# Re-timing block sums and gate-weight sums in the second half of layer one of a linear-attention and gMLP kernel

## Chip, cores and metric

The kernel runs on one core of one Trainium2 chip. The metric is device time in microseconds of one execution. Engines go by the profile's names: PE is TensorE, DVE is VectorE, ACT is ScalarE, POOL is GpSimd, and SP is the engine whose queue issues most of the transfers (DMAs).

## The reference

Four blocks follow each other on a 2048 x 512 tensor in float32: attention block A, gMLP block B, and both once more with the same weights. "Layer one" is the first A and B.

```python
x = x + _A_ref(_layernorm(x), A_wqkv, A_wo)
x = x + _B_ref(_layernorm(x), B_w_in, B_w_sp, B_b_sp, B_w_out)
...
def _A_ref(x, wqkv, wo):          # H = 32 heads of 16
    q, k, v = ...                 # x @ wqkv
    pq, pk = phi(q), phi(k)       # where(t > 0, t + 1, exp(t)) + 1e-6
    kv = einsum("bhsd,bhse->bhde", pk, v)
    z = einsum("bhsd->bhd", pk)
    o = einsum("bhqd,bhde->bhqe", pq, kv) / (einsum("bhqd,bhd->bhq", pq, z)[..., None] + 1e-6)
    return o.reshape(B, S, D) @ wo
def _B_ref(x, w_in, w_sp, b_sp, w_out):    # Fh = 896
    z = gelu(x @ w_in)
    z1, z2 = z[..., :Fh], layernorm(z[..., Fh:])
    g = einsum("ts,bsf->btf", w_sp, z2) + b_sp[None, :, None]
    return (z1 * g) @ w_out
```

## The kernel before

**Numbers.** Each float32 matrix is held as two halves: `high` (line 134, ACT) rounds it, `low` (137, DVE) takes the rest. A product is three matmuls (`mm3`, 147): high by high, high by low, low by high.

**Block products.** The large product with `w_sp` (2048 x 2048) and part of the product with `w_in` are computed with seven products of blocks in place of eight, so sums of blocks are needed as operands. The *block sums* of `w_sp` are made by `Sums` (1172): for each of 16 pieces it loads three 128 x 512 tiles (a21, a22, a11), makes three sums on POOL, a21 + a22, a21 + a11 and (a21 + a22) + a11 (`add`, 1206), and stores them to DRAM for the later stage `P4`. `fetch` (1183) issues the three loads, `store` (1197) the three stores, `tick` (1210) does one piece's share of a step. Eight of the pieces are made in the loop below, the rest in layer one's `P4`, where `tick` is called as well. The *gate-weight sums* are those of `w_in`'s first half: `Make` (203) handles three groups g. From the step `MAKE_AT[g]` on it loads two tiles, one step later makes four half-width adds on DVE (`add`, lines 215 to 218), then splits one tile on ACT and DVE in each of two steps and stores each a step later (`store`, 226).

**The loop.** The second half of layer one's attention and the first product of its gMLP run in `P2.run` (1081), in steps s of one row tile (128 rows) each. In the order in which they are recorded, step s does the following from s = 6 on:

- issue loads of x for row s + 1 and of the turned query row (`qturn.load`), and the stores of the last sums (`sums.store()`)
- b(s): DVE transposes the query row (line 330), ACT and DVE split it
- den: three short DVE operations (805 to 807) for row s + 2
- c(s - 1): 12 matmuls, then DVE adds the residual (846) and takes statistics (264, 266), whose root is taken on POOL (268 to 273)
- `a2_mul` (814, DVE), `c3`: ACT normalises the row (279), which is stored turned (yt, through `xturn`); `a` (793) is a multiplication on POOL
- d(s - 2): DVE transposes the turned row that was loaded in the step before, ACT and DVE split it into a quarter of a `qd` tile (`d_high`, `d_low`). In steps 14 and on `d_high` comes before `c3`
- e(s - 3): 24 matmuls of width 448, GELU on ACT (902); e4(s - 4) normalises an earlier row on ACT (279), and DVE takes a difference (913) when that row is below 8; e3 takes statistics, with a root on POOL
- f: up to two groups of 12 matmuls of width 512, each with a GELU on ACT (927) and a store of its output. There are two groups in most steps, one in steps 9 and 13, none in 14
- from step 14 on `side` gives six or twelve block-product matmuls (993 to 995) a step
- `make.step(s)`, one split of the gate weights (`w1.piece`, POOL takes the rest until step 7), then `sums.tick` and `xturn.load(s - 1)`

e(s - 3) in step s reads what d wrote in step s - 1, and c(s - 1) reads what b wrote in step s - 1.

**What sets the order.** The kernel is recorded by hand: each engine runs its instructions in the order written, and waits on semaphores. SP issues its transfers in the same way, so a transfer that waits holds all behind it. A transfer from SP also waits, beside its data, for the eighth before it.

**Where things lie.** Tiles `pg` (pages, 128 x 512) come from 23 slots, the one that was given back longest ago first, `lag` putting a page further back. A `z` tile of a row holds its query row first, then, by `ztag`, a sum's tile ("sum"), a GELU output ("out"), a turned row ("turn") and at last the row's z. `TOKEN_TICKS` names the steps in which sums are made and the z tile that takes the first of the three loaded tiles; the other two are pages. `SPARE_TAGS` names the z tile for the second GELU output of a step; without an entry it is a page.

Before, `tick(s)` stands at the end of step s: it stores what is made, loads the tiles for step s + 1 if that is in `TOKEN_TICKS`, and makes the sums of step s. The loads of a step thus stand in SP's queue ahead of `xturn.load(s - 1)`, and POOL makes the sums of step s behind all its other work of that step:

```python
w1.piece(True)
w1.fetch()
if self.L == 0:
    sums.tick(s, TOKEN_TICKS)
self.xturn.load(s - 1)
```

Of the kernel before, what the change touches and what calls it, by code (L numbers as in the profile page):

```python
# [25 lines left out]
PHI_EPS = 1e-6  # L26
DEFER = 6
STORE, POOL = 6, 3
TOKEN_TICKS = {at: (at,) for at in (5, 6, 8, 9, 11, 12, 13, 14)}
SPARE_TAGS = {6: 7, 8: 7, 9: 10, 11: 10, 14: 15, 16: 15}  # L30
MIX_TICKS = (2, 4, 7, 8, 10, 12, 14, 16, 20, 21, 23, 24, 26, 27, 29, 30, 32, 34, 35, 37, 38, 39, 40, 41)
MIX_UNITS = (11, 15, 18, 20, 25, 31, 36, 40), (1, 3, 5, 7, 9, 11, 13, 15)
MAKE_AT = 5, 8, 11
ROW_UNITS = range(1, 9)
INNER_UNITS = range(47, 55, 2)
FIRST_AT = ("N1", 4), ("N1", 7), ("N2", 1), ("N2", 2), ("N2", 4), ("N1", 10)
# [54 lines left out]
def mixer_kernel(ctx: ExitStack, tc: tile.TileContext, x_in, wqkv, wo_d, win1_d, win2_d, wsp_d, bsp_d, wout_d,  # L91
# [111 lines left out]
    class Make:  # L203
# [29 lines left out]
        def step(self, i):  # L233
            for g in range(3):
                at = i - MAKE_AT[g]
                if at == 0:
# [98 lines left out]
    class P1:  # L335
# [227 lines left out]
        def run(self):  # L563
            side = deque()
            for w in (self.wo, self.win2):
                side.extend([w] * len(w.pieces))
            if self.L == 0:
                self.first(side)
            else:
                self.second(side)  # L570
# [201 lines left out]
    class P2:  # L772
# [308 lines left out]
        def run(self, sums):  # L1081
            w1 = self.win1
            own = inner["N1"]
            make = Make() if self.L == 0 else None
            for s in range(1, NT + 3):
                self.loadx(s + 1)
                self.qturn.load(s + 1)
                if self.L == 0:
                    sums.store()
                if s in self.qturn.by_pe:  # L1090
                    self.c(s - 1)
                    self.b_high(s)
                    self.c2(s - 1)
                    self.b_low(s)
                    self.c_stats(s - 1)
                    if s >= 2:
                        self.d_high(s - 2)
                        self.d_low(s - 2)
                    self.p1.late()
                    self.c3(s - 1)  # L1100
                    self.a2(s + 2)
                    self.p1.late_phi()
                    self.a(s + 3)
                elif s - 2 in self.xturn.by_pe:
                    self.b_high(s)
                    self.c(s - 1)
                    self.c2(s - 1)
                    self.c_stats(s - 1)
                    self.a2_den(s + 2)
                    self.b_low(s)  # L1110
                    self.a2_mul(s + 2)
                    self.d_high(s - 2)
                    self.d_low(s - 2)
                    self.c3(s - 1)
                    self.a(s + 3)
                else:
                    if s < NT:
                        self.b_high(s)
                    self.a2_den(s + 2)
                    if s < NT:  # L1120
                        self.b_low(s)
                    if s <= NT:
                        self.c(s - 1)
                        self.c2(s - 1)
                        self.c_stats(s - 1)
                    if s == NT:
                        quads.put(*self.W2)
                        pages.put(self.zbc)
                    self.a2_mul(s + 2)
                    sooner = s >= 14  # L1130
                    if sooner and s <= NT + 1:
                        self.d_high(s - 2)
                    if s <= NT:
                        self.c3(s - 1)
                    self.a(s + 3)
                    if s <= NT + 1:
                        if not sooner:
                            self.d_high(s - 2)
                        self.d_low(s - 2)
                if s >= 15:  # L1140
                    self.block_sums()
                if 4 <= s <= 6:
                    self.e3(s - 4)
                if 5 <= s <= 7:
                    self.e4(s - 5)
                if s > 6:
                    self.e4(s - 4)
                if s >= 3:
                    self.e(s - 3)
                    self.e2(s - 3)  # L1150
                if s >= 6:
                    self.e3(s - 3)
                self.f(s + 2)
                self.f(SPARE_TAGS.get(s) if self.L == 0 else None)
                self.side(s)
                if self.L == 0:
                    make.step(s)
                elif s == 5:
                    own.begin(2)
                elif 6 <= s:  # L1160
                    own.staged()
                self.fq.extend(self.fnext)
                self.fnext = []
                w1.piece(True)
                w1.fetch()
                if self.L == 0:
                    sums.tick(s, TOKEN_TICKS)
                self.xturn.load(s - 1)
            self.win2.free()


    class Sums:
# [37 lines left out]
        def tick(self, i, at):  # L1210

            self.store()
            if i + 1 in at:
                self.fetch(at[i + 1] if isinstance(at, dict) else ())
            if i not in at:
                return
            k, j, fourth = self.todo.popleft()
            if fourth:
                s2, a12 = self.raw.popleft()
                self.add(4, k, j, a12, s2, a12, s2)  # L1220
            else:
                a21, a22, a11 = self.raw.popleft()
                self.add(1, k, j, a22, a21, a22)
                self.add(3, k, j, a21, a21, a11)
                self.add(2, k, j, a11, a22, a11)
# [641 lines left out]
    sums = Sums()  # L1867
# [45 lines left out]
```

## Time and profile before

| | |
|---|---|
| median of 3 runs | 1369.9 us (1369.87 to 1370.38) |
| the profiled execution | 1370.94 us |
| its span, first to last instruction | 1369.2 us |
| mean granted TensorE clock | 0.999 |
| DMA traffic | 310.18 MB, mean 227 GB/s |
| sums made in the loop (line 1207) | 24 of 1.3 to 1.4 us |

The span is one execution as the hardware profiler saw it, the time of the run is a little longer than it. A group or timeline row names line, engine, operation, output and inputs by the program's tile names, and in brackets the idle time of the engine before it with what ended it. A row of a table by stretches gives its length and the busy time of PE, PE's weight loads, DVE, ACT and POOL with the number of instructions, then the granted clock, the DMA engines' busy share and GB/s.

### The profile page before, as it was taken

The numbers are of one execution on the slowest core, as the hardware profiler recorded it, in microseconds if no ns is written. First come the engines' busy times: TensorE is split into PE (matmuls) and PEld (weight loads), VectorE is DVE, ScalarE is ACT, GpSimd is POOL, SyncE is SP. The second block draws the span as 40 slices with busy tenths as digits, with TensorE's granted clock in tenths as the row PEclk, the third lists the DMA queues.
The fourth block names the chain that finished last, engine by engine and source line by source line (L and its number), as shares of the span: only waits on it lengthen the run. The fifth ranks groups of instructions, "written<-read, shape, count | busy, mean of one in ns | idle before, by whom it ended". The sixth has DMA issues, their size and how long they took to land.

```text
span 1369.2 us, 18313 instructions
## 1 busy us (share of the span) xinstructions
PE 1358.0 (99%) x6087; PEld 1132.8 (83%) x6087; DVE 1030.3 (75%) x1582; ACT 638.2 (47%) x1021; POOL 470.9 (34%) x551
## 2 busy tenths in 40 slices
PE   9999999989999999999999999999999999999998
PEld 7888888878888888878888888888888888888887
DVE  7985888777855888886678768887767798978642
ACT  6775544436542343432456655444455534533310
POOL 2333474463144237426421133633230011412340
PEclk9999999999999999999999999999999999999999
DMA  5762388886698988895686533666668798568652
GB/s 180 236 214 88 123 277 272 272 270 195 213 303 281 307 270 282 274 376 181 216 260 201 189 106 115 209 200 208 192 196 279 226 336 322 188 198 304 228 184 90
DMA packets 184496, 310.18 MB, mean 227 GB/s; under 512 B 15696, under 2 KB 67920, under 8 KB 180304
## 3 DMA queue, kind: packets, MB, share of 16 engines
q1 hardware_dynamic: 172736, 262.73, 59.0%
q0 software_dynamic: 8064, 39.85, 8.2%
q10 hardware_dynamic: 3600, 6.42, 1.3%
q8 instruction: 48, 0.79, 0.2%
q14 instruction: 48, 0.39, 0.1%
HBM read 211.68 MB, written 97.26 MB: 226 GB/s over the span
## 4 chain that ended last, share of the span: by engine, by line
PE 76%; DVE 3%; DMA 3%; ACT 1%; issue 1%; POOL 0%; SPq 0%; DVEq 0%; ACTq 0%; POOLq 0%
PE bank L151 12%; PE bank L150 12%; PE bank L149 12%; PE bank L1613 9%; PE bank L1615 9%; PE bank L1614 9%; PE bank L1544 3%; PE bank L1546 3%; PE bank L1547 3%; PE bank L995 1%; PE bank L993 1%; PE bank L994 1%; DMA qd<-n 1%; DMA pg<-qt 0%; DVE st L264 0%
## 5 line engine op out<-in xcount | busy, mean ns | idle before, releaser
L1613 PE MATMUL bank<-qd,pg 128*128 128x512 f32 x544 | 211.6, 389 | 0.0
L1614 PE MATMUL bank<-qd,pg 128*128 128x512 f32 x544 | 211.6, 389 | 0.0
L1615 PE MATMUL bank<-qd,pg 128*128 128x512 f32 x544 | 211.6, 389 | 0.0
L1460 DVE TENSOR_TENSOR qd<-qd,qd 128x1024 fp32r<-128x1024 f32 x104 | 144.4, 1388 | 70.3 <-ACT qd L1451 70.2
L1451 ACT ACTIVATE qd<-qd 128x1024 fp32r<-128x1024 f32 x104 | 110.1, 1058 | 137.5 <-DVE qd L1460 42.5
L151 PE MATMUL bank<-qd,pg 128*128 128x512 f32 x380 | 148.6, 391 | 0.5 <-DVE pg L138 0.5
L135 ACT ACTIVATE pg<-pg 128x512 fp32r<-128x512 f32 (+1 forms) x146 | 89.4, 621 | 121.4 <-DVE pg L330 46.4
L268 POOL TENSOR_SCALAR rs<-mv 128x1 f32<-128x1 f32 x95 | 42.3, 446 | 267.5 <-DVE mv L266 253.3
L1635 POOL TENSOR_TENSOR bg<-bg,pg 128x512 f32<-128x512 f32 x56 | 92.2, 1657 | 109.5 <-DMA pg<-z 104.0
L138 DVE TENSOR_TENSOR pg<-pg,pg 128x512 fp32r<-128x512 f32 (+1 forms) x143 | 111.2, 778 | 15.1 <-ACT pg L135 13.8
L1615 PEld LDWEIGHTS bank<-qd,pg 128*128 128x128 f32 x544 | 102.1, 188 | 21.3
L1614 PEld LDWEIGHTS bank<-qd,pg 128*128 128x128 f32 x544 | 102.1, 188 | 21.3
L1613 PEld LDWEIGHTS bank<-qd,pg 128*128 128x128 f32 x544 | 102.1, 188 | 21.0
L1207 POOL TENSOR_TENSOR pg<-pg,pg 128x512 f32<-128x512 f32 x48 | 72.2, 1505 | 135.4 <-DMA pg<-in_wsp_dram 93.2
L149 PE MATMUL bank<-qd,pg 128*128 128x512 f32 x284 | 110.9, 390 | 0.1
L150 PE MATMUL bank<-qd,pg 128*128 128x512 f32 x284 | 110.6, 389 | 0.0
L330 DVE STREAM_TRANSPOSE pg<-pg 128x512 f32<-128x512 f32 x79 | 86.3, 1092 | 16.9 <-DMA pg<-yt 11.2
L149 PE MATMUL bank<-bg,qd 128*128 128x448 f32 x256 | 95.1, 372 | 3.9 <-ACT qd L135 3.6
L151 PE MATMUL bank<-bg,qd 128*128 128x448 f32 x256 | 94.5, 369 | 0.2
L150 PE MATMUL bank<-bg,qd 128*128 128x448 f32 x256 | 94.3, 368 | 0.0
L1544 PE MATMUL bank<-qd,pg 128*128 128x512 f32 x224 | 87.5, 390 | 0.5 <-DMA qd<-n 0.5
L1546 PE MATMUL bank<-qd,pg 128*128 128x512 f32 x224 | 87.4, 390 | 0.3 <-DVE qd L1460 0.3
(220 smaller groups left out, 3194.0 us busy)
## 6 DMA issues: line engine op xcount, KB each, us to landing
qd<-s SPq DMA_DIRECT2D x64, 512.0 KB, 4.1
qd<-n POOLq DMA_DIRECT2D x32, 1024.0 KB, 8.3
pg<-in_wsp_dram SPq DMA_DIRECT2D x91, 256.0 KB, 4.7
qd<-in_wsp_dram SPq DMA_DIRECT2D x40, 512.0 KB, 4.4
s<-pg SPq DMA_DIRECT2D x56, 256.0 KB, 4.7
pg<-z SPq DMA_DIRECT2D x56, 256.0 KB, 4.0
n<-pg SPq DMA_DIRECT2D x55, 256.0 KB, 4.6
x<-pg SPq DMA_DIRECT2D x48, 256.0 KB, 2.7
```

Of the source, the lines that this page charges most:

```text
L138: nc.vector.tensor_sub(l, src, h.bitcast(F32))
L149: nc.tensor.matmul(out, ah, bh, start=start, stop=False)
L150: nc.tensor.matmul(out, ah, bl, start=False, stop=False)
L151: nc.tensor.matmul(out, al, bh, start=False, stop=stop)
L1451: nc.scalar.activation(wh, r, AF.Copy)
L1460: nc.vector.tensor_sub(wl, r, wh.bitcast(F32))
L1544: m(out[i], h[:, o, f], w[:, o, 0], start=first and name in ("P1", "P2", "P5"), stop=False, skip_group_check=True)
L1546: m(out[i], h[:, o, f], w[:, o, 1], start=False, stop=False, skip_group_check=True)
L1613: m(out, h[:, o], w[:, 0, j, :], start=start, stop=False, skip_group_check=True)
L1614: m(out, h[:, o], w[:, 1, j, :], start=False, stop=False, skip_group_check=True)
L1615: m(out, l[:, o], w[:, 0, j, :], start=False, stop=stop, skip_group_check=True)
L1635: nc.gpsimd.tensor_tensor(u, u, z1, op=OP.mult)
```

## The change

Three constants change, and the order at two places of the loop.

- `TOKEN_TICKS`: sums are made in steps 5 to 12, one piece a step, where it was 5, 6, 8, 9, 11, 12, 13 and 14.
- `Sums.tick` is cut in two: the new `Sums.sum` makes the sums. The loop calls it in the middle of step s, behind `a` and d and ahead of e4 and e3, so that POOL has them between `a` and the statistics of e3.
- The loads for the sums of step s + 1 are issued by the loop itself at the end of step s, behind `xturn.load(s - 1)` where they stood ahead of it. The stores stay at the start of the next step.
- `SPARE_TAGS` loses steps 6, 8, 9 and 11: z tiles 7 and 10 now take sums' tiles, and the second GELU output of steps 6, 8 and 11 is a page (step 9 has only one).
- `MAKE_AT`: 5, 8, 11 becomes 5, 7, 9. Make's loads are issued in steps 5, 7 and 9, its adds fall in steps 6, 8 and 10 (before 6, 9, 12), its splits in 7 and 8, 9 and 10, 11 and 12 (before 7 and 8, 10 and 11, 13 and 14), its last store in step 13 (before 15).

In `P4` of layer one `tick` is called as before and does the same as before. The matmuls and their order are the same.

```diff
-TOKEN_TICKS = {at: (at,) for at in (5, 6, 8, 9, 11, 12, 13, 14)}
-SPARE_TAGS = {6: 7, 8: 7, 9: 10, 11: 10, 14: 15, 16: 15}
+TOKEN_TICKS = {at: (at,) for at in range(5, 13)}
+SPARE_TAGS = {14: 15, 16: 15}
-MAKE_AT = 5, 8, 11
+MAKE_AT = 5, 7, 9
@@ in P2.run, after d
+                if self.L == 0:
+                    sums.sum(s, TOKEN_TICKS)
                 if s >= 15:
                     self.block_sums()
@@ in P2.run, at the end of a step
                 w1.piece(True)
                 w1.fetch()
-                if self.L == 0:
-                    sums.tick(s, TOKEN_TICKS)
                 self.xturn.load(s - 1)
+                if self.L == 0 and s + 1 in TOKEN_TICKS:
+                    sums.fetch(TOKEN_TICKS[s + 1])
@@ class Sums, in tick
             self.store()
             if i + 1 in at:
-                self.fetch(at[i + 1] if isinstance(at, dict) else ())
+                self.fetch()
+            self.sum(i, at)
+
+        def sum(self, i, at):
+
             if i not in at:
                 return
             k, j, fourth = self.todo.popleft()
```

## The prediction

> **What bounds the kernel now.** I read the page first, then TensorE's idle time row by row, then engine times cut at the steps of the changed loop (`P2.run`, layer one), then the queue and VectorE around each loss.
>
> ```profile
> span 1369.2 us, 18313 instructions
> PE 1358.0 (99%) x6087; PEld 1132.8 (83%) x6087; DVE 1030.3 (75%) x1582; ACT 638.2 (47%) x1021; POOL 470.9 (34%) x551
> ```
>
> TensorE is idle for 1369.2 - 1358.0 = 11.2 us in all, so a schedule change that leaves every matmul in place can win only that and time lost to a slow clock. Next, the steps; each row starts at the first matmul of c in steps 8 to 15 (columns: length, then busy time of PE, PEld, DVE, ACT, POOL, clock, DMA share, GB/s).
>
> ```profile
> 205.51:218.56 13.05, 13.05 (x61) 11.27 (x60) 9.85 (x18) 7.58 (x13) 4.97 (x8) 1.00 0.71 236
> 218.56:228.90 10.34, 10.34 (x50) 9.02 (x49) 9.21 (x14) 2.98 (x6) 5.75 (x8) 1.00 0.80 257
> 228.90:242.78 13.88, 13.69 (x62) 11.11 (x61) 11.37 (x19) 4.46 (x7) 7.10 (x9) 1.00 0.93 324
> 242.78:256.53 13.75, 13.57 (x61) 11.11 (x60) 10.38 (x18) 6.13 (x11) 5.80 (x11) 1.00 0.71 231
> 256.53:269.58 13.05, 13.05 (x61) 11.27 (x60) 8.83 (x16) 5.38 (x10) 8.28 (x11) 1.00 0.84 273
> 269.58:279.92 10.34, 10.34 (x50) 9.01 (x49) 8.68 (x14) 4.13 (x7) 5.28 (x6) 1.00 0.97 332
> 279.92:291.70 11.78, 9.68 (x43) 7.65 (x42) 8.74 (x14) 4.88 (x8) 4.74 (x8) 1.00 0.91 296
> 291.70:305.73 14.03, 12.42 (x50) 10.19 (x48) 9.53 (x15) 4.86 (x8) 8.85 (x11) 0.88 0.72 238
> ```
>
> Step 8 has one group f of 12 matmuls more than step 9: 13.05 - 10.34 = 2.71 us, and so e takes 10.34 - 2 x 2.71 = 4.92. With its 18 wide matmuls step 14 needs 1.5 x 2.71 + 4.92 = 8.99, step 15 10.34, steps 10 and 11 13.05. Lost: 0.83, 0.70, 2.79 and 3.69 us in steps 10, 11, 14, 15: 8.0 in all. These are what the change can move.
>
> ```profile
> 245.78 0.47 PE L149 MATMUL bank<-bg,qd 128*128 128x448 f32 x1
> 246.51 0.47 PE L151 MATMUL bank<-bg,qd 128*128 128x448 f32 x1
> 245.76 0.69 DVE L138 TENSOR_TENSOR qd<-pg,qd 128x512 fp32r<-128x512 f32 x1 [1.51 <-ACT qd L135]
> 285.04 0.47 PE L149 MATMUL bank<-bg,qd 128*128 128x448 f32 x1 [2.05 <-ACT qd L135]
> 296.14 0.47 PE L149 MATMUL bank<-bg,qd 128*128 128x448 f32 x1 [1.56 <-ACT qd L135]
> 298.00:301.40 3.40, 3.40 (x11) 3.05 (x10) 3.05 (x5) 1.68 (x4) 1.38 (x3) 0.50 0.94 281
> ```
>
> The two large losses are e waiting for d of the step before, for its rounded half from ScalarE. In step 11 it is e too: its third matmul (L151) starts at 246.51, just behind d's rest from VectorE (245.76 + 0.69 = 246.45). Step 15 also lost 3.40 x 0.50 = 1.7 us to half clock. Why d is late, in the queue and on VectorE:
>
> ```profile
> 276.57 1.10 SPq L1193 DMA_DIRECT2D pg<-in_wsp_dram  x2
> 277.77 0.41 SPq L131 DMA_DIRECT2D pg<-yt  x1
> 283.23 1.09 DVE L330 STREAM_TRANSPOSE pg<-pg 128x512 f32<-128x512 f32 x1 [0.73 <-DMA pg<-yt]
> 285.02 0.69 DVE L138 TENSOR_TENSOR qd<-pg,qd 128x512 fp32r<-128x512 f32 x1 [0.70 <-ACT qd L135]
> ```
>
> The turned row yt is loaded behind three block-sum loads, lands 283.23 - 277.77 = 5.5 us after issue, and d ends at 285.7, while e could have begun at 283.0.
>
> **The change part by part.** Nothing is added or taken out: 24 sums on GpSimd, their 24 loads and 24 stores, twelve VectorE adds and the splits move. What they cost is how much longer they make VectorE's round: from the query row's transposition in one step to that in the next.
>
> ```profile
> 210.16 1.11 DVE L330 STREAM_TRANSPOSE pg<-pg 128x512 f32<-128x512 f32 x1
> 221.54 1.09 DVE L330 STREAM_TRANSPOSE pg<-pg 128x512 f32<-128x512 f32 x1
> 230.10 1.10 DVE L330 STREAM_TRANSPOSE pg<-pg 128x512 f32<-128x512 f32 x1 [1.66 <-DMA pg<-yt]
> 234.71 0.37 DVE L215 TENSOR_TENSOR pg<-pg 128x256 f32<-128x256 f32 x1
> 236.03 0.42 DVE L218 TENSOR_TENSOR pg<-pg 128x256 f32<-128x256 f32 x1
> 236.38 1.11 DVE L330 STREAM_TRANSPOSE pg<-pg 128x512 f32<-128x512 f32 x1
> 238.00 1.28 DVE L806 TENSOR_TENSOR den<-den,zeps 128x32 f32<-128x32 f32 x1
> 239.58 1.56 DVE L138 TENSOR_TENSOR pg<-pg,pg 128x512 fp32r<-128x512 f32 x1
> 249.78 1.08 DVE L330 STREAM_TRANSPOSE pg<-pg 128x512 f32<-128x512 f32 x1
> 251.37 0.19 DVE L806 TENSOR_TENSOR den<-den,zeps 128x32 f32<-128x32 f32 x1
> 251.87 0.63 DVE L138 TENSOR_TENSOR pg<-pg,pg 128x512 fp32r<-128x512 f32 x1
> 257.11 0.69 DVE L138 TENSOR_TENSOR qd<-pg,qd 128x512 fp32r<-128x512 f32 x1 [1.46 <-ACT qd L135]
> 258.14 0.56 DVE L913 TENSOR_TENSOR z_z<-z_z 128x384 f32<-128x384 f32 x1 [0.34 <-ACT z_z L279]
> 260.49 0.72 DVE L138 TENSOR_TENSOR pg<-pg,pg 128x512 fp32r<-128x512 f32 x1 [0.48 <-ACT pg L135]
> 261.14 1.09 DVE L330 STREAM_TRANSPOSE pg<-pg 128x512 f32<-128x512 f32 x1
> ```
>
> Step 11's round, which met no sum: 261.14 - 249.78 = 11.36, of it 0.48 + 0.72 = 1.2 for Make's split: base 10.2. L913 with its wait is 0.9 and is absent from step 12 on: 9.3 there. Make's adds: 236.38 - 234.71 = 1.7. A sum that meets the round's front: (1.28 - 0.19) + (1.56 - 0.63) = 2.0. Step 9's round, 236.38 - 221.54 = 14.84, is 10.2 + 1.7 + 2.0 and half of the 1.66 us wait for yt.
>
> *Sums at mid-step.* GpSimd would take them behind `a`, into this hole:
>
> ```profile
> 237.94 1.29 POOL L1207 TENSOR_TENSOR z_sum<-z_sum,pg 128x512 f32<-128x512 f32 x1
> 239.30 1.29 POOL L1207 TENSOR_TENSOR pg<-pg,pg 128x512 f32<-128x512 f32 x1
> 255.67 1.29 POOL L793 TENSOR_TENSOR pg<-z_q,pg 128x512 f32<-128x512 f32 x1
> 260.18 0.22 POOL L268 TENSOR_SCALAR rs<-mv 128x1 f32<-128x1 f32 x1 [3.21 <-DVE mv L266]
> ```
>
> L806 at 238.00 ended at 239.28, just behind the sum that ended at 239.23; the L138 from 239.58 outlasted the sum that ended at 240.59. So I take it that such an operation is held until the running sum ends. In step 11 a first sum from 257.0 to 258.3 holds d's L138 (257.11) by 1.2 us, the next one L913 by some 0.7: 1.9 a round. Bounds: 0 (the sums' loads land when VectorE is elsewhere) and 4.0 (three sums of 1.29 end to end, two gaps of 0.07). I take 1.9, from the row it hits. From step 12 on the hold is covered by the wait for ScalarE's GELU. The Trainium skill (SBUF — State Buffer, Who interferes with whom) states it harder: a VectorE instruction with two SBUF inputs contends with a GpSimd one that reads SBUF, and who comes second waits for the whole instruction. The rows agree (1.28 against 0.19); by it alone every two-input operation under those 4.0 us could lose a full 1.29, which speaks for the upper bound.
>
> *Steps 12 to 15.* No loads stand ahead of yt, no sums in the fronts of 13 to 15, no adds in 12, no splits in 13 and 14, and stores of sums no longer hold SP there. Rounds 9.3 + 1.2 = 10.5 and 9.3 against TensorE's 13.05 and 10.34: the losses of 14 and 15 go, 2.79 + 3.69 = 6.5 us, if the lag at step 13 allows it.
>
> *Steps 8 to 11.* Steps 7 and 10 get sums they hadn't, adds come in 8 and 10, splits in 7 to 12. (Steps 5 to 7 lost nothing and I leave them so: each front is rid of a sum, 2.0, and each middle gets one, 1.9.) Rounds: 10.2 + 1.9 + 1.2 + 1.7 = 15.0 in 8 and 10, 13.3 in 9 and 11. VectorE's lag behind TensorE at step 8 is 210.16 - 205.51 = 4.65. d ends 257.80 - 249.78 = 8.0 after a round's start, with the hold 9.2; e's third matmul comes two pitches (0.4) in, so 8.8 counts. Step 9: lag 4.65 + 15.0 - 13.05 = 6.6, room 10.34 + 2.71 - 8.8 = 4.25: TensorE waits 2.35 in step 10. Step 10, now 15.4 long: lag 6.6 + 13.3 - 10.34 = 9.55, room 15.4 + 2.71 - 8.8 = 9.3: it waits 0.25 in step 11. Step 11, 13.3 long: lag 9.15, room 7.2: 1.95 in step 12. Step 12, 15.0 long: lag 9.15, room 8.9: 0.25 in step 13. Step 13, 10.6 long: lag 9.15 + 10.5 - 15.0 = 4.65, room without a hold 10.6 + 2.71 - 7.6 = 5.7: it holds. New losses 4.8 for the old 1.5: +3.3.
>
> *Pages.* The second GELU output of steps 6, 8 and 11 goes to a page instead of a z tile, and b's low half takes the page whose store was issued last:
>
> ```profile
> z<-pg SPq DMA_DIRECT2D x13, 256.0 KB, 2.2
> ```
>
> 2.2 us after a store issued about when the round starts, b's L138 (251.87 - 249.78 = 2.1 in) waits 0 to 0.5: nothing taken. If it is late, c waits next, with 13.05 - 2.7 us of cover. SP's z stores, Make's loads and stores stay ahead of yt; the x and qt loads fall no further behind.
>
> Sum: 1370.94 (profiled execution; 1.7 lies outside its span) - 6.5 + 3.3 = 1367.7. That execution is 1.0 above the median of the runs shown, so 1369.9 - 3.2 = **1366.7 us**.
>
> **Rivals.** (1) All of it goes: sums meet only covered operations (hold near 0, rounds 11.4 to 13.1 within slack). For: GpSimd's 3.21 us hole and a yt load sooner by 277.77 - 276.57 = 1.2 us and the third load's issue. Against: adds and splits stand closer. 1369.9 - 8.0 = 1361.9. (2) The queue takes over: steps 7 to 11 now issue 16, 16, 17, 16, 16 transfers of 256 KB, 21.2 MB in 62.5 us of TensorE work: 340 GB/s, where the fullest quoted step ran at 332 with a share of 0.97. At 332 they need 63.9: 1.4 more, yt late again: 1368.1. Against: step 13 lost nothing at that rate. (3) Slower: three sums hold VectorE for their whole 4.0 us in steps 8 to 11; 2.1 more in four rounds adds 8.4: 1366.7 + 8.4 = 1375.1. It decides from a hold of 1.9 + 3.2/4 = 2.7 on. Against: transpositions, statistics and the PSUM add between them keep their times in the rows. A new stall could also bring back the half clock, +1.7: 1368.4. The Trainium skill (TensorE: Matmul & The Clock Gate, What's actually happening) ties that to an idle window of about 3.4 us; here it came after gaps of 2.05 and 1.56, so the row decides and the case stays in the range.
>
> **How the numbers follow.** Chances: forecast 0.36, all gone 0.27, queue 0.22, slower 0.15. A time within 0.2% (2.7 us) of 1369.9 counts as no change, about what this measurement can tell. Faster: 0.27 and three quarters of 0.36: 0.54, with a little of the queue's case 0.56. Same: 0.29. Slower: 0.15. Range 1361.8 (all gone) to 1371.2 (a hold of 3.0, just past break-even); likeliest case alone 1364.5 to 1368.5.
>
> **What would show it.** Right: steps 14 and 15 at 9.0 and 10.3 us with clock 1.00; no wait of VectorE on yt there; sums between `a` and e's statistics; steps 10 and 12 some 2 us over 13.05, e waiting on `qd L138`; L138 of d at 1.5 to 1.9 us in steps 7 to 11. Wrong: steps 8 to 12 at 13.05 (hold too dear, rival 1), yt landing 6 us after issue with a DMA share near 1.0 (rival 2), L913, adds and d all stretched (rival 3), or any loss left in step 14.

## The result and the profile after

| | before | after |
|---|---|---|
| median | 1370.2 us (8 runs, 1369.85 to 1371.03) | 1365.88 us (8 runs, 1365.55 to 1366.85) |
| span of the profiled execution | 1369.2 us | 1363.8 us |

The ratio is 0.9969 (95% interval 0.9958 to 0.998): 4.3 us faster, where 3.2 were forecast. The page of the changed kernel, its span and first engines:

```profile
span 1363.8 us, 18322 instructions
PE 1354.6 (99%) x6087; PEld 1133.0 (83%) x6087; DVE 1033.3 (76%) x1582; ACT 637.9 (47%) x1021; POOL 473.7 (35%) x551
```

Every engine runs as many instructions as before. What moved is where TensorE waits. Steps 10 to 15 of the changed kernel, in the columns of the table by stretches (length, busy time of PE, PEld, DVE, ACT, POOL, clock, DMA share, GB/s):

```profile
228.76:246.14 17.38, 15.06 (x62) 12.36 (x60) 14.12 (x22) 7.12 (x11) 11.96 (x15) 0.90 0.93 317
246.14:259.19 13.05, 13.05 (x61) 11.27 (x60) 11.36 (x20) 4.36 (x10) 7.62 (x11) 1.00 1.01 351
259.19:272.24 13.05, 13.05 (x61) 11.26 (x60) 11.29 (x17) 6.07 (x11) 9.05 (x11) 1.00 0.88 300
272.24:282.58 10.34, 10.34 (x50) 9.01 (x48) 9.24 (x15) 3.71 (x8) 6.17 (x9) 1.00 1.02 349
282.58:291.55 8.97, 8.97 (x43) 7.89 (x42) 5.71 (x10) 3.97 (x7) 1.90 (x6) 1.00 0.81 264
291.55:301.88 10.33, 10.33 (x49) 9.01 (x48) 6.79 (x11) 4.73 (x8) 2.34 (x7) 1.00 0.34 106
...
234.50:237.90 3.40, 3.26 (x9) 2.92 (x10) 3.37 (x6) 1.32 (x3) 3.06 (x3) 0.50 0.61 208
```

Steps 14 and 15 went from 11.78 and 14.03 us to 8.97 and 10.33: the forecast 6.5 us, to the tenth. Steps 11 to 13 lose nothing. Only step 10 does: 17.38 - 13.05 = 4.33 us, of it 3.40 x 0.50 = 1.7 in a stretch at half clock. TensorE's rows there:

```profile
232.99 0.47 PE L149 MATMUL bank<-bg,qd 128*128 128x448 f32 x1 [1.35 <-ACT qd L135]
...
234.64 0.74 PE L151 MATMUL bank<-bg,qd 128*128 128x448 f32 x1 [0.97 <-DVE qd L138]
```

This is e, waiting for both halves of the d of step 9. VectorE's timeline on the way there (rounds 8 and 9, from one query row's transposition to the next):

```profile
210.90 1.09 DVE L330 STREAM_TRANSPOSE pg<-pg 128x512 f32<-128x512 f32 x1
...
218.93 1.65 DVE L138 TENSOR_TENSOR qd<-pg,qd 128x512 fp32r<-128x512 f32 x1 [1.51 <-ACT qd L135]
220.51 1.64 DVE L913 TENSOR_TENSOR z_z<-z_z 128x384 f32<-128x384 f32 x1
...
225.65 1.08 DVE L330 STREAM_TRANSPOSE pg<-pg 128x512 f32<-128x512 f32 x1
...
232.97 1.61 DVE L138 TENSOR_TENSOR qd<-pg,qd 128x512 fp32r<-128x512 f32 x1 [1.51 <-ACT qd L135]
234.50 1.63 DVE L913 TENSOR_TENSOR z_z<-z_z 128x384 f32<-128x384 f32 x1
...
237.91 1.09 DVE L330 STREAM_TRANSPOSE pg<-pg 128x512 f32<-128x512 f32 x1
```

GpSimd's timeline of the same kernel beside the operations from 232.97 on:

```profile
232.75 1.28 POOL L1209 TENSOR_TENSOR pg<-z_sum,pg 128x512 f32<-128x512 f32 x1
234.11 1.60 POOL L1209 TENSOR_TENSOR z_sum<-z_sum,pg 128x512 f32<-128x512 f32 x1
235.79 1.47 POOL L1209 TENSOR_TENSOR pg<-pg,pg 128x512 f32<-128x512 f32 x1
```

d's L138 starts at 232.97 in the middle of a sum that ends at 234.03, and ends 0.55 us behind that, at 234.58: it is held until the sum is done. L913 then meets the next sum. The two took 0.69 and 0.56 before. Step 9 began at 218.42, so VectorE's lag there (start of the query row's transposition less start of c) is 225.65 - 218.42 = 7.23 us, where the prediction's room is 4.25.

### The profile page after: what moved, and what is told of

Read it like the earlier page. It is cut to its first block, busy times and chain, and to the rows that moved or that the text cites. A ratio compares the mean times of both kernels' runs of the same rounds, so it can differ in the third digit from the quotient of the medians.

```text
span 1363.8 us, 18322 instructions
## 1 busy us (share of the span) xinstructions
PE 1354.6 (99%) x6087; PEld 1133.0 (83%) x6087; DVE 1033.3 (76%) x1582; ACT 637.9 (47%) x1021; POOL 473.7 (35%) x551
## 4 chain that ended last, share of the span: by engine, by line
PE 92%; DVE 4%; ACT 2%; DMA 1%; issue 1%; POOL 0%; SPq 0%; DVEq 0%; ACTq 0%; POOLq 0%
PE bank L151 17%; PE bank L149 16%; PE bank L150 16%; PE bank L1619 9%; PE bank L1620 9%; PE bank L1621 9%; PE bank L1552 4%; PE bank L1553 4%; PE bank L1550 4%; PE bank L995 1%; PE bank L994 1%; PE bank L993 1%; PE bank L736 1%; DVE st L264 1%; DVE pg L138 1%
## 5 line engine op out<-in xcount | busy, mean ns | idle before, releaser
L138 DVE TENSOR_TENSOR pg<-pg,pg 128x512 fp32r<-128x512 f32 (+1 forms) x143 | 106.9, 748 | 14.4 <-ACT pg L135 11.9
```

What stands on the lines that cost most here:

```text
L138: nc.vector.tensor_sub(l, src, h.bitcast(F32))
```

## Experiments

Four questions: which of the two moves gains; what the three constants do; whether the sums or the gate-weight work put VectorE behind; whether a version without step 10's loss can be had. Times are medians, the difference is against the kernel before on the same chip.

### One move at a time

The kernel before, with the loads moved alone (e1), the sums moved alone (e2), and both (e5, e10):

```diff
 e1:            w1.fetch()
+               self.xturn.load(s - 1)
+               sums.fetch(TOKEN_TICKS[s + 1])    # if s + 1 in TOKEN_TICKS
+               sums.sum(s, TOKEN_TICKS)
-               sums.tick(s, TOKEN_TICKS)
-               self.xturn.load(s - 1)
 e2: behind d:
+               sums.sum(s, TOKEN_TICKS)
     and at the end of the step:
-               sums.tick(s, TOKEN_TICKS)
+               sums.fetch(TOKEN_TICKS[s + 1])    # if s + 1 in TOKEN_TICKS
                self.xturn.load(s - 1)
 e5, e10 = e2, but at the end of the step
                self.xturn.load(s - 1)
                sums.fetch(TOKEN_TICKS[s + 1])
```

> The kernel before with one edit: a step's block-sum loads are issued behind the turned row yt, not ahead of it; ticks, place of the sums and gate-weight steps are those of before. Theory (VectorE's rounds set the loss): only the waits on yt go (0.73 us in step 14, most of 1.66 in step 9), the sums still hold each next round's front by 2.0 us, so steps 14 and 15 still lose over 3 us together: 1368 to 1369.5. Rival (the queue order alone is the gain): steps 14 and 15 come to 9.0 and 10.3 us, 1370.2 - 6.5 = 1363.7.

> The kernel before with one edit: the sums are issued mid-step, behind a and d; loads still ahead of yt, ticks and gate-weight steps of before. Theory (rounds): fronts are rid of 2.0 us, but in steps 13 and 14 yt still lands 5.5 us after issue and VectorE now waits for it longer, so half of the 6.5 us of steps 14 and 15 stays: 1366 to 1368. Rival (the place of the sums is everything): 1370.2 - 6.5 = 1363.7. Rival (queue order is everything): 1370.

> The kernel after with its three constants as before (ticks 5, 6, 8, 9, 11 to 14, the spare tiles, gate-weight steps 5, 8, 11): only the two moves stay, sums mid-step and loads behind yt. Theory (rounds): no sum in steps 7 and 10, so the lag at step 9 is 4.3 and step 10 loses 0.1; sums, splits and the short steps 13 and 14 meet, so step 15 loses 1.2 to 2.4: 1363.4 to 1364.6. Rival (each move only hides the same stall, and the ticks out of steps 13 and 14 are what count): steps 14 and 15 still lose over 4: 1366.5.

> Only the two moves (sums mid-step, loads behind yt), the three constants of before: a second look at the fastest version. Theory: the loop loses nothing again, 7 us under before and 2.7 under after: 1363.1. Rival (the first look was a lucky placing of yt's load in steps 13 and 14): one of them loses 1 or more: 1364 to 1365.

| | median | difference | ratio, 95% interval |
|---|---|---|---|
| e1 loads | 1366.18 | -3.9 | 0.9972 (0.9962 to 0.9981) |
| e2 sums | 1366.82 | -3.2 | 0.9976 (0.9967 to 0.9986) |
| e5 both | 1363.14 | -7.0 | 0.9953 (0.9937 to 0.9968) |
| e10 both | 1362.22 | -7.3 | 0.9944 (0.9931 to 0.9958) |

The two are worth about the same and add up. e1 gave 3.9 us where I expected 0.7 to 2.2: I had counted only the waits for yt of 1.66 and 0.73 us and overlooked the longest, in round 12 of the kernel before:

```profile
269.39 1.09 DVE L330 STREAM_TRANSPOSE pg<-pg 128x512 f32<-128x512 f32 x1 [2.64 <-DMA pg<-yt]
```

It cost TensorE nothing on the spot, but it put round 13 that much later. In e1 none of these waits is left, and steps 14 and 15 lose 0.85 each where they lost 2.8 and 3.7 (table by stretches of e1). Not all of that is gained: the steps behind them, up to the end of the loop, take 29.3 us in e1 and 26.9 in after.

```profile
278.87:288.69 9.82, 9.47 (x43) 7.73 (x42) 6.78 (x11) 4.86 (x8) 4.71 (x8) 1.00 0.88 280
288.69:299.88 11.19, 10.83 (x49) 8.86 (x48) 7.12 (x11) 4.97 (x8) 6.69 (x10) 1.00 0.94 298
```

In e2 the sums are out of the fronts, VectorE comes sooner and waits longer for yt, which still lands behind three loads. Its profile is of the slowest of the ten runs (1368.87 us); step 14 lost 4.75 us in it, 1.7 of that at half clock. VectorE's timeline of e2, rounds 12 to 14:

```profile
268.42 1.09 DVE L330 STREAM_TRANSPOSE pg<-pg 128x512 f32<-128x512 f32 x1 [3.06 <-DMA pg<-yt]
...
282.30 1.09 DVE L330 STREAM_TRANSPOSE pg<-pg 128x512 f32<-128x512 f32 x1 [2.81 <-DMA pg<-yt]
293.26 1.09 DVE L330 STREAM_TRANSPOSE pg<-pg 128x512 f32<-128x512 f32 x1 [1.66 <-DMA pg<-yt]
```

With both, nothing is lost in steps 8 to 15, where I had expected 1.2 to 2.4 in step 15. Behind them, against the 26.9 us of after, e5 loses 0.4 us and e10 1.6. The table by stretches of e5, steps 10, 14 and 15:

```profile
228.47:241.53 13.06, 13.06 (x62) 11.27 (x60) 11.69 (x19) 3.93 (x7) 8.00 (x11) 1.00 0.99 343
...
277.97:286.94 8.97, 8.97 (x43) 7.89 (x42) 7.40 (x11) 4.25 (x8) 5.23 (x8) 1.00 0.92 313
286.94:297.27 10.33, 10.33 (x49) 9.01 (x48) 6.41 (x11) 4.86 (x8) 6.57 (x10) 1.00 0.88 300
```

### The constants

The kernel after, with the gate-weight steps of before (e3), with the ticks and spare tiles of before (e11), and unchanged (e9):

```diff
 e3
-MAKE_AT = 5, 7, 9
+MAKE_AT = 5, 8, 11
 e11
-TOKEN_TICKS = {at: (at,) for at in range(5, 13)}
-SPARE_TAGS = {14: 15, 16: 15}
+TOKEN_TICKS = {at: (at,) for at in (5, 6, 8, 9, 11, 12, 13, 14)}
+SPARE_TAGS = {6: 7, 8: 7, 9: 10, 11: 10, 14: 15, 16: 15}
```

> The kernel after with one edit: the gate-weight sums' steps are again 5, 8, 11. Theory (rounds): round 8 loses its adds (1.7 us), so the lag at step 9 falls from 7.2 to 5.5 and step 10's loss from 4.3 us to some 1.3; the splits back in steps 13 and 14 cost 1.2 in step 15: 2.5 lost in the loop, 1365.9 - 1.8 = 1364.1. Rival (moving the gate-weight work is what cleared steps 14 and 15): they lose 6.5 again and step 10 gets 3 back: 1369.4.

> The kernel after with the ticks and spare tiles of before (5, 6, 8, 9, 11 to 14), gate-weight steps 5, 7, 9 kept. Theory (lag): step 7 has no sum, so the lag at step 9 falls by 1.2 from 7.2 to 6.0 and step 10 loses 1.8, without the half clock: after's 4.3 becomes 1.8 to 2.2: 1363.4 to 1363.8. Rival (gate-weight steps 7 and 9 cost 2.2 us whatever the ticks): 1363.1 + 2.2 = 1365.3.

> The kernel after, unchanged, beside the three others on one chip. Both theories: 1365.9, 4.3 us under before, and step 10 loses 4.3.

| | ticks | gate weights | median | difference | ratio, 95% interval |
|---|---|---|---|---|---|
| e10 | old | old | 1362.22 | -7.3 | 0.9944 (0.9931 to 0.9958) |
| e3 | new | old | 1363.69 | -6.4 | 0.996 (0.9945 to 0.9975) |
| e11 | old | new | 1364.33 | -5.2 | 0.996 (0.9948 to 0.9973) |
| e9 | new | new | 1364.96 | -4.6 | 0.9963 (0.995 to 0.9975) |

e9, e10 and e11 ran beside each other on one chip: after is 1364.96 - 1362.22 = 2.7 us slower than the moves alone, and no run of the one reaches the other's (1364.4 to 1365.04 against 1361.8 to 1362.79). So the constants give back part of what the moves gain. The new gate-weight steps alone cost 2.1 us (e11 against e10), the new ticks alone 0.6 to 1.0 (e3 against e5 and e10, by their differences, since e3 and e5 ran on another chip). e9 was expected to lose 4.3 us in step 10 and lost 2.82, without the half clock. In e3 step 10 lost 1.17 us, as expected from a lag of 5.47; of the 1.2 expected in step 15, 0.2 came. The table by stretches of e3:

```profile
228.72:242.94 14.22, 13.33 (x61) 11.19 (x60) 12.44 (x20) 4.34 (x7) 9.09 (x12) 1.00 1.01 337
```

In e11 the time lies between the two expectations (1363.4 to 1363.8, and 1365.3), and the places fit neither: step 10 lost 0.67, not 1.8, and step 15 lost 11.39 - 10.34 = 1.05. VectorE's timeline of e11 shows what stood ahead of that second loss: in round 14 the transposition of yt, at 288.96, had waited 2.21 us for yt, whose load was issued at 285.62, where e5 issued it at 283.46 and VectorE did not wait. Why that load was issued later stays open.

### What puts VectorE behind

The kernel after with sums left out in steps 7 to 9 (e6) or in step 9 alone (e12):

```diff
             a21, a22, a11 = self.raw.popleft()
+            if isinstance(at, dict) and 7 <= i <= 9:       # e12: i == 9
+                self.made += [(1, k, j, a22, ()), (3, k, j, a21, ()), (2, k, j, a11, ())]
+                return
```

> The kernel after with the nine GpSimd sums of steps 7, 8 and 9 left out of the computation (their loads and stores stay, so that unsummed tiles are stored). Theory (the sums hold VectorE, 1.2 us net a round and 0.96 on d's own last operation): the lag at step 9 falls from 7.2 to 4.8 and d takes 8.0, so step 10 loses nothing, 4.3 less than after: 1361.6. Rival (the adds and splits crowded into round 8, 2.9 us, make the lag by themselves and the holds are covered): step 10 still loses 2 to 4: 1364 to 1366.

> The kernel after with only the three GpSimd sums of step 9 left out of the computation (loads and stores stay). Theory (lag gathered in rounds 7 and 8, 7.2 at step 9): d of step 9 is 0.96 faster, but still late: step 10 loses 1.4 to 2.0: 1363.3 to 1364. Rival (the sum that holds d's last operation in step 9 is the whole stall): step 10 loses nothing: 1361.6.

e6: 1362.42 us, -7.7, ratio 0.9944 (0.9928 to 0.996); e12: 1363.19 us, -6.4, ratio 0.9952 (0.994 to 0.9965). VectorE's timeline of e6, rounds 8 and 9 with what was held in after:

```profile
209.10 1.09 DVE L330 STREAM_TRANSPOSE pg<-pg 128x512 f32<-128x512 f32 x1
...
216.45 0.69 DVE L138 TENSOR_TENSOR qd<-pg,qd 128x512 fp32r<-128x512 f32 x1 [1.31 <-ACT qd L135]
217.48 0.56 DVE L913 TENSOR_TENSOR z_z<-z_z 128x384 f32<-128x384 f32 x1 [0.34 <-ACT z_z L279]
...
219.83 0.69 DVE L138 TENSOR_TENSOR pg<-pg,pg 128x512 fp32r<-128x512 f32 x1 [0.48 <-ACT pg L135]
...
222.18 1.09 DVE L330 STREAM_TRANSPOSE pg<-pg 128x512 f32<-128x512 f32 x1
...
233.55 1.09 DVE L330 STREAM_TRANSPOSE pg<-pg 128x512 f32<-128x512 f32 x1 [0.21 <-DMA qt<-pg]
```

Without sums L138 and L913 are back at 0.69 and 0.56, round 8 takes 222.18 - 209.10 = 13.08 where after took 225.65 - 210.90 = 14.75, and the loop loses nothing. Step 10 of e12, from the table by stretches:

```profile
228.78:243.75 14.97, 13.57 (x62) 11.11 (x61) 11.55 (x21) 6.15 (x11) 6.65 (x11) 1.00 0.91 306
```

In e12 d of step 9 was no longer held, but the lag was as large (7.21 us) and step 10 still lost 1.92. So most of the loss is the lag that had gathered, and the hold on d itself adds the rest, 2.82 - 1.92 = 0.9. Both the sums and the gate-weight adds make that lag: without the sums of steps 7 to 9 it is 4.00 (e6), without the adds of round 8 it is 5.47 (e3).

Nine profiles follow the same rule. Expected is the lag at step 9 less the prediction's room (4.25; 5.45 where step 9 has no sums), measured is the length of step 10 less 13.05:

| | lag at step 9 | expected loss | measured |
|---|---|---|---|
| after | 7.23 | 2.98 | 2.6 and 1.7 of half clock |
| e9, after again | 7.22 | 2.97 | 2.82 |
| e3 | 5.47 | 1.22 | 1.17 |
| e8 | 5.25 | 1.00 | 0.91 |
| e7 | 5.24 | 0.99 | 1.07 |
| e11 | 4.98 | 0.73 | 0.67 |
| e5 | 3.24 | 0 | 0 |
| e12, no sums in 9 | 7.21 | 1.76 | 1.92 |
| e6, no sums in 7 to 9 | 4.00 | 0 | 0 |

e10 fits too (lag 3.12, nothing lost). e2 does not: its lag was 3.57 and step 10 lost 0.63. There the transposition of yt in round 9 had itself waited 2.38 us for yt, so the rule holds only where yt has landed in time.

The opposite edit has the sums of after issued at the end of a step again (e4):

```diff
 behind d:
-               sums.sum(s, TOKEN_TICKS)
 at the end of the step, behind the loads:
+               sums.sum(s, TOKEN_TICKS)
```

> The kernel after with one edit: the sums of a step are issued at its end again, so that they meet the next round's front; ticks, load order and gate-weight steps of after. Theory (rounds): a front is held by 2.0 us in each of steps 6 to 13, where the mid-step hold was 1.9 gross and 1.2 net of covered waits: lags grow by 0.8 a round, step 10 loses 5 to 6, step 9 one, steps 12 and 14 two each: 1370 to 1373. Rival (only the ticks and the load order count): 1366.

1369.64 us, -0.4, ratio 0.9996 (0.9987 to 1.0005): next to nothing is left. That is just under the expected 1370 to 1373: steps 9, 10, 12 and 14 lost 7.9 us, not 10 to 11. The sums there meet the gate-weight adds too, 0.42 us each when free:

```profile
223.30 1.54 DVE L216 TENSOR_TENSOR pg<-pg,pg 128x256 f32<-128x256 f32 x1
224.88 1.40 DVE L217 TENSOR_TENSOR pg<-pg,pg 128x256 f32<-128x256 f32 x1
226.31 1.40 DVE L218 TENSOR_TENSOR pg<-pg 128x256 f32<-128x256 f32 x1
```

### Two attempts to keep the ticks and lose nothing

The kernel after with the gate-weight work taken out of round 8 by starting it earlier (e7), and its end later as well (e8):

```diff
-MAKE_AT = 5, 7, 9
+MAKE_AT = 4, 8, 11      # e8: 4, 8, 12
```

> The kernel after with gate-weight steps 4, 8, 11: adds in steps 5, 9, 12, splits in 6 and 7, 10 and 11, 13 and 14. Theory (rounds): no gate-weight work in round 8, so the lag at step 9 is 3.8 to 4.3, inside the 4.25 that step 10 allows: steps 8 to 12 lose nothing, step 15 at most 0.9: 1361.5 to 1362.5. Rival (the adds, 1.7 us, fall into step 5 of 8.1 us, where VectorE's round is 8.5 already): steps 6 and 7 lose a microsecond or two: 1363.5 to 1365.

> As the run with gate-weight steps 4, 8, 11, but the last of the three at 12: adds in 13, splits in 14 and 15. Theory (rounds): adds leave round 12 (11.2), and step 13, with no sum behind it and no split, carries 1.7 at 11.0; lag 3.7 at step 14: nothing lost in the loop: 1361.6. Rival (the splits in 14 and 15 meet the short steps): step 15 or 16 loses 1 to 2: 1363.

Both missed. e7: 1364.0 us, -6.1, ratio 0.9959 (0.9946 to 0.9972), no better than e3; e8: 1368.23 us, -1.9, ratio 0.9987 (0.9978 to 0.9996). e7's rival had the right mechanism and the wrong place. VectorE in step 5 of e7:

```profile
181.00 1.51 DVE L215 TENSOR_TENSOR pg<-pg 128x256 f32<-128x256 f32 x1
182.55 1.40 DVE L216 TENSOR_TENSOR pg<-pg,pg 128x256 f32<-128x256 f32 x1
183.98 0.43 DVE L217 TENSOR_TENSOR pg<-pg,pg 128x256 f32<-128x256 f32 x1
...
184.78 1.09 DVE L330 STREAM_TRANSPOSE pg<-pg 128x512 f32<-128x512 f32 x1
```

The adds meet the sums of step 5 and are held, and round 6 begins at 184.78 where it began at 181.01 in after. Nothing is lost in steps 6 to 9, but rounds of 12.5 to 13.9 us against steps of 13.05 work hardly any of the 3.8 us off, and the short step 9 presents the bill: 1.07 us in step 10. In e8 the last split, recorded at the end of step 15, is queued on ScalarE behind the work of the block product that has begun by then. VectorE's timeline of e8 in step 16 (its own half of that split):

```profile
308.26 0.69 DVE L138 TENSOR_TENSOR pg<-pg,pg 128x512 fp32r<-128x512 f32 x1 [2.29 <-ACT pg L135]
```

The residual and the statistics of step 16 stand behind it, so d is late and TensorE waits in step 17:

```profile
312.24 0.74 PE L149 MATMUL bank<-bg,qd 128*128 128x448 f32 x1 [2.52 <-ACT qd L135]
```

A stretch at half clock goes with it, in the table by stretches:

```profile
312.00:315.40 3.40, 3.16 (x9) 2.67 (x10) 3.11 (x7) 2.78 (x5) 0.00 (x0) 0.50 0.46 142
```

The version that beats both kernels is thus e5 (run again as e10): the two moves with the constants of before.

## Why the prediction was right, and where it was off

- **Steps 12 to 15, -6.5.** Right, with its reasons: no sums in the fronts of 13 to 15 and no wait for yt that counts (one of 0.69 us is left in step 14, and TensorE does not feel it). With the constants of before, e1 and e2 show that both moves were needed; with those of after only the sums' place was taken back (e4, step 14 lost 2.1), and no run takes back the loads' place alone.
- **New losses, step 10 first.** Right in place and cause. Without half clock step 10 lost 2.82 us (e9) where 2.35 stood in the sum. The profiled execution lost 4.33, the 1.7 that the prediction kept for the range.
- **New losses in 11 to 13: 0.25, 1.95, 0.25.** Wrong: 0 in the profile, 0.30 in step 12 of e9. The step that failed is the hold of 1.9 us a round. Gross it was even 2.04, (1.65 - 0.69) + (1.64 - 0.56), but it takes the place of two waits for ScalarE, 0.34 ahead of L913 and 0.48 ahead of the split, which were in the quoted rows and which I left in the base. Net, rounds 8 and 9 of after are 14.75 - 13.08 = 1.67 and (237.91 - 225.65) - (233.55 - 222.18) = 0.89 longer than in e6 (1.10 without e6's wait of 0.21). The larger of the two holds a second thing, 0.88 - 0.19 = 0.69 us of L806 in the front of round 8: behind the sums of step 7, GpSimd came late to its gate-weight split (L143), which in e6 ended ahead of L806 and in after ran beside it. So the hold in the middle of a round is about 1.0 net, half of the 1.9. The bases themselves were exact (13.1 and 11.4 by the prediction's terms without a hold). So the rounds of 15.0, 13.3, 15.0 and 13.3 were 14.75, 12.26, 14.03 and 12.33, and VectorE caught up behind step 10. The half clock of step 10 helped it to: the lag at step 11 was 5.80 in after and 7.34 in e9, which lost the 0.30. The two rows of after, from VectorE's and GpSimd's timelines:

```profile
212.50 0.88 DVE L806 TENSOR_TENSOR den<-den,zeps 128x32 f32<-128x32 f32 x1
212.04 1.29 POOL L143 TENSOR_TENSOR bg<-pg,bg 128x512 fp32r<-128x512 f32 x1
```

- **Steps 5 to 7 left as they were.** Off the other way: step 7 makes sums that it did not make before, round 7 takes two of L913, and both were held. So the lag at step 8 was 210.90 - 205.37 = 5.53, not 4.65 (without sums in step 7 it was 3.95 in e5 and 3.98 in e6), and that made step 10's loss larger than forecast.
- **Sum.** In the profiles the loop gave 4.0 us (its tail starts at 328.80 instead of 332.78), against 3.2 forecast. That they lie so close is partly luck: steps 11 to 13 lost 2.45 less than forecast and step 10 1.98 more (4.33 for 2.35), the half clock included, so that new losses of 4.3 stand where 4.8 were forecast. Of the remaining 1.4 us, 1.0 lies around two waits of before that after does not have. Some of the experiments have one or two like them and some have none, whichever of the moves they have; where they come from stays open:

```profile
609.36 0.47 PE L1544 MATMUL bank<-qd,pg 128*128 128x512 f32 x1 [0.24 <-DMA qd<-n]
612.60 0.47 PE L1544 MATMUL bank<-qd,pg 128*128 128x512 f32 x1 [0.25 <-DMA qd<-n]
```

- **Rivals.** All gone: not with the constants of after, since the hold is real; it is nearly what e5 shows with the constants of before, and e6 without the sums of steps 7 to 9. The queue: step 11 ran at 351 GB/s with a share of 1.01, step 13 at 349 and 1.02, above the 332 that the rival took as the ceiling, and neither lost anything. Slower: it needed a hold of 2.7 net, measured were 0.9 to 1.7 in the rounds that e6 frees, L806 included.
- **The hold and the port.** The Trainium skill (SBUF — State Buffer, Who interferes with whom) makes the shared port an exclusive lock and says that the order of issue decides who waits. The runs agree: L138 0.69 against 1.61 to 1.66 us, and GpSimd's sums waited in their turn, 1.60 and 1.47 us against 1.28. By the rule alone every two-input operation under the sums could have been held; in the middle of rounds 8 to 11 only two a round were, because statistics follow, and they keep their times (1.14 us in after and in e6).
- **Not tried.** The pages: b's L138, which the prediction saw at risk, waits for nothing in after's rounds 8 to 13, and no run separates the pages from the ticks.

## What to carry to other kernels

Where a loop's steps have unequal lengths, follow the second engine's lag from step to step: a delay may cost nothing where it arises and be paid behind the next short step. In e7 a hold of step 5 was paid in step 10. When work of GpSimd is moved beside VectorE's, count the hold net of the waits that it replaces, and look at which two-input operations it newly meets. And take a change of several edits apart: here two moves gained 7 us and the constants that came with them gave 2.7 back.

## What the runs showed of the hardware

The half clock did not follow from the length of a wait. The same two waits in step 10 (1.35 and 0.97 us in after, 1.35 and 0.98 in e9) were followed by 3.40 us at 0.50 in one execution and by full clock in the other. TensorE's rows of e9:

```profile
232.96 0.47 PE L149 MATMUL bank<-bg,qd 128*128 128x448 f32 x1 [1.35 <-ACT qd L135]
...
234.60 0.47 PE L151 MATMUL bank<-bg,qd 128*128 128x448 f32 x1 [0.98 <-DVE qd L138]
```

And its step 10, with a mean clock of 1.00, from the table by stretches:

```profile
228.73:244.60 15.87, 13.54 (x62) 11.11 (x60) 13.25 (x21) 5.59 (x10) 10.47 (x14) 1.00 0.91 298
```

One wait of 1.99 us in e4 had no such stretch either, and in e8 the stretch began at 312.00, before the matmul that had waited resumed at 312.24. The Trainium skill (TensorE: Matmul & The Clock Gate, What's actually happening) has a free-running window of about 3.4 us; a phase that differs between executions would fit these rows, but no run here fixed the phase. All four stretches in the loop (before, after, e2 and e8) lasted 3.40 us, but none of the waits ahead of them was as long as that, 2.52 us at most: a window that was idle throughout was not needed.
